# Three passes of a two-layer kernel over token blocks of 384 instead of 288

## The chip, the cores and the metric

One NeuronCore of a Trainium2 chip runs the whole program. The metric is the device time of one execution in microseconds, as the median of several. The core has a matrix engine (TensorE, PE in the profile; its weight loads are listed as PEld), VectorE (DVE), ScalarE (ACT), GpSimd (POOL) and SyncE (SP), which here issues nearly all DMAs.

## The reference

```
attention, B=4, H=8, S=576, D=64, 32 packing queries p per head:
  packed = softmax(p k^T / 8) v          32 x 64 for each head and batch
  x      = softmax(q packed^T / 8) packed          -> 2304 tokens x 512
layer one:  h = x  @ w_in   (512 x 2048);  g = softplus(h);  x1 = g @ w_out   (2048 x 512)
layer two:  h = x1 @ w_in2  (512 x 2048);  g = h*sigmoid(h); y  = g @ w_out2
```

The weights come as 64-bit floats, and the kernel turns them into 32-bit ones from their integer halves. The result is a float32 array of 2304 x 512.

## The kernel before

**Precision.** In most products both operands are split into a rounded part and a remainder (fp32r, one matmul each), and three of the four products are summed: low x high, high x low, high x high.

**Layer one** never builds x. Since x is the second softmax (A, 576 tokens x 32 packing slots x 8 heads, so two row tiles of 128) times `packed`, the kernel multiplies `packed` into w_in first. `packed(b, qs)` makes, for one batch b and some column tiles of w_in, the weights `vw` by small fp32 matmuls (64 x 32 tiles of the array, eight of them side by side, L523) in a two-bank PSUM tile. ScalarE then rounds them out of PSUM (L531) and VectorE makes the remainder (L535). These weights differ from batch to batch. `ax` holds A, rounded and remainder, for all 2304 tokens.

**Passes, units, steps.** The 16 tiles of the hidden dimension (128 each, index j) are taken in four passes of four (`GJ = 4`). In each pass the 2304 tokens are taken in eight blocks of 288, so two blocks make a batch of 576. A unit is one pass and one block, and has four steps, one for each j. A step in `run_steps` does, in this order on TensorE: `emit_in`, the six matmuls of the hidden tile h (L557); a pack call if one is due; `emit_out`, twelve matmuls (L606) that add the unit before, four j times three products, to one of the four 128-row tiles of the output. So every full step has 18 matmuls, each with a 128 x 128 weight load of its own and, for its moving side, the columns of the block. ScalarE takes softplus (L569) and the rounded part gh (L570), VectorE the remainder gl (L574) and the sum of y into `ya` (L622). The hidden tile stays in its PSUM bank until gl is made; there are two such banks.

**What sets the order.** Pass one is a script written out by hand, which also holds the attention. Passes two to four are a loop over steps: 32 a pass, `base(f) = 32 f`. The rest hangs on step numbers in tables: `vstep` says when a pack call runs (for each batch one wide call of 512 columns, two steps ahead of its first block), `when` the conversion of layer one's weights for the next pass, `I2` and `O2` the conversion of layer two's weights, which are made meanwhile and stored to DRAM (`wd`, `od`, `td`), `plan_load` the DMAs at the end of a step. Within a step, `go(point)` lets such jobs put their instructions into each engine's order at a named place (A0 before the step's ScalarE work, A2 behind it, D0, D1, D, D2 on VectorE). Every engine runs its instructions in the order in which they were put, and SP its DMAs likewise.

**Layer two's weights.** A pair of `raw` tiles becomes eight sums in `wf`; `high_i` rounds (L238) and `low_i` (GpSimd, L244) makes remainders into `whl2`, one buffer for all seven products, stored by `store_i` with one DMA of 1792 KB. Output weights go through `ohl` (`high_o`, `low_o`, `store_o`: one DMA of 512 KB) and sums in `tmp` (`t_store`, 1024 KB).

**The change of layers.** From step 24 of the last pass (`XC0`) the staging memory is given up for layer two's operands `xc`, which `x_split` makes from `ya` at steps 24, 25 and 29, its low parts a step later; layer two's first weights are loaded at steps 23 and 24. Layer two (`second`, blocks of 384 tokens) takes the last unit's four output groups into its first step (`last_out`).

Of the kernel before, what the change touches and what calls it, by code (L numbers as in the profile page):

```python
# [28 lines left out]
N0 = 288  # L29
BLOCKS = [(c, N0) for c in range(0, T, N0)]  # L30

# [17 lines left out]
def body(ctx, tc, kT, vv, qT, pT, wi1, wo1, wi2, wo2, out):  # L49
# [5 lines left out]
    dram = pool("dram", 1, space=bass.MemoryType.DRAM)  # L55
    l0_stack, att_stack, stage_stack, psa_stack = (ExitStack() for _ in range(4))
# [456 lines left out]

    def packed(b, qs):
        yield "PE"
        t = two_banks()
        wide = len(qs) > 1
        for k in range(NK):
            w = whl["i", 2 * qs[0] + (k if wide else k // 2)]
            w = w if wide else w[:, (k % 2) * 256:(k % 2 + 1) * 256]  # L520
# [8 lines left out]
        for i, q in enumerate(qs):  # L529
            v = l0.tile([P, 2, NR, 256], F32R, name="vw", bufs=3)  # L530
            nc.scalar.activation(out=v[:, 0], in_=t[:, :, 256 * i:256 * i + 256], func=AF.Copy)  # L531
            vs.append(v)
        yield "D"
        for i, (q, v) in enumerate(zip(qs, vs)):
            nc.vector.tensor_tensor(  # L535
                out=v[:, 1], in0=t[:, :, 256 * i:256 * i + 256], in1=v[:, 0].bitcast(F32), op=ALU.subtract
            )
            vw[b, q] = v

# [3 lines left out]
    def emit_in(s):  # L543
        u, i = steps[s]
        js, blk = units[u]
        j = js[i]
        c, n = BLOCKS[blk]
        cols = slice(c, c + n)
        h = ps.tile([P, 512], F32, name="h")[:, :n]
        v = vw[blk // 2, j // 2]  # L550
        fs = slice((j % 2) * P, (j % 2 + 1) * P)
        mm = [
            (v[:, vp, r, fs], ax[:, ap * NR + r, cols])
            for vp, ap in ((1, 0), (0, 1), (0, 0)) for r in range(NR)
        ]
        for i, (w, x) in enumerate(mm):
            nc.tensor.matmul(h, lhsT=w, rhs=x, start=(i == 0), stop=(i == len(mm) - 1))  # L557
        return h

    def act_scalar(s, h):  # L560
        if s < 2 * GJ:
            gf = g0.tile([P, N0], F32, name="gf", tag="gh")
# [3 lines left out]
        gh = g0.tile([P, N0], F32R, name="gh")  # L566
        gl = g0.tile([P, N0], F32R, name="gl")
# [105 lines left out]

    I2 = (1, 5), (10, 14), (20, 22), (32, 33), (43, 49), (54, 57), (64, 67), (77, 78)
    O2 = 3, 6, 13, 15, 23, 25, 30, 36, 45, 46, 60, 63, 73, 74, 81, 83

    when = {}
    vstep = {(b, (i,)): 8 * b - 4 + i for b in range(B) for i in range(2)}
    vstep[0, (1,)] = 3
    del vstep[0, (0,)]  # L680
    for f in range(1, NPASS):
        for b in range(B):
            vstep[b, (2 * f, 2 * f + 1)] = base(f) + 8 * b - 2

    def last_use(k, n):
        f = n // GJ
        if k == "o":
            return base(f) + PER + GJ
        return vstep[B - 1, (2 * f, 2 * f + 1) if f else (n // 2,)]

    def plan_all():

        for f in range(1, NPASS - 1):
            for d, s in enumerate((7, 9, 26, 29)):
                when["i", GJ * f + GJ + d] = base(f) + s
            for d, s in enumerate((12, 19, 16, 24)):
                when["o", GJ * f + GJ + d] = base(f) + s
        for (k, n), s in when.items():
            ring = RING[k]
            free = last_use(k, n - ring)  # L700
            load = max(s - 5, free)
# [6 lines left out]
        for m, (s, k, n) in enumerate(use):  # L708
            free = use[m - RAW][0] if m >= RAW else 0
            plan_load(lambda k=k, n=n: load_raw(k, n), base(1) + max(free, s - 5))  # L710
        for jp, s in enumerate(I2):
            a, b = (base(1) + x for x in s)
            plan(Item(conv_pair(jp)), (a, b, b + 3, b + 4))
            plan_load(lambda jp=jp: store_i(jp), b + 8)
        for n, s in enumerate(O2):
            s += base(1)
            plan(Item(conv_o(n)), (s, s + 1) + (s + 3,) * (n % 2))
            plan_load(lambda n=n: store_o(n), s + 4)
            if n % 2:
                plan_load(lambda n=n: t_store(n), s + 4)  # L720
        for q, s in (Q1, 24), (Q2, 25), (Q4, 24), (Q5, 25), (Q7, 29), (Q6, 29), (Q3, 29):
            s += base(3)
            plan(Item(x_split(0, q)), (s, s + 1))
        for t in range(RI):
            plan_load(lambda t=t: load_i1(t), base(3) + 23)
        for r in range(GJ):
            plan_load(lambda r=r: load_s(r), base(3) + 24)

# [47 lines left out]
    def first_pass():  # L776
        items, made, ys = {}, {}, {}
        for b in range(B):
            items[f"a1.{b}"] = Item(att1(b))
            for i in range(2):  # L780
                items[f"a2.{2 * b + i}"] = Item(att2(2 * b + i))
                items[f"v.{b}.{i}"] = Item(packed(b, (i,)))
        items["v.0.2.3"] = Item(packed(0, (2, 3)))
        for n in range(2 * GJ):
# [477 lines left out]
```

## Time and profile before

| | |
|---|---|
| median of 3 runs | 724.73 us (724.57 to 725.1) |
| profiled execution | 724.65 us, its span 722.9 us |
| TensorE busy | 716.0 us (99%), 5330 matmuls |
| VectorE, ScalarE, GpSimd busy | 72%, 55%, 55% |
| passes two to four | 117.9 to 361.4 us of the span |
| layer two | from 361.4 us on |

A line of a group gives: source line, engine, operation, output<-input, shape, count, then busy time, the mean duration of one in ns, idle time of the engine just before and what ended it. A timeline line gives the start, how long the merged run of instructions lasted, engine, source line and count. Matmuls are pipelined: one starts before the one ahead has ended, so that spacing is read from the starts of neighbours and not from durations.

### The profile page before, as it was taken

How to read it: one execution, taken by the hardware profiler on the slowest of the kernel's cores; microseconds unless marked ns; L12 is line 12 of the kernel's file. 1: busy time of each engine (PE TensorE's matmuls, PEld its weight loads, DVE VectorE, ACT ScalarE, POOL GpSimd, SP SyncE). 2: the span in 40 equal slices, each digit the busy share in tenths (PEclk: the TensorE clock that was granted, in tenths of full speed). 3: DMA queues.
4: the chain of work that ended last, by engine and by line, in shares of the span. 5: the costliest groups of instructions: out<-in, count | busy, mean ns of one | idle time of the engine just before them, and what ended most of it. 6: DMA issues, size and time to landing. Idle time of an engine off the chain costs nothing.

```text
span 722.9 us, 14127 instructions
## 1 busy us (share of the span) xinstructions
PE 716.0 (99%) x5330; PEld 685.5 (95%) x5330; DVE 520.7 (72%) x937; ACT 394.3 (55%) x789; POOL 397.5 (55%) x352
## 2 busy tenths in 40 slices
PE   8999999999999999999999999999999999999998
PEld 6878999999899999999999999999999999999997
DVE  4888888888878887575845567787557786645557
ACT  3677887767765766556636534443644363444341
POOL 0122110857753746456027567689656769765655
PEclk9999999999999999999999999999999999999999
DMA  9946151587687664485739878778978787987732
GB/s 337 365 166 228 69 193 39 197 328 302 261 318 269 241 244 194 146 306 220 261 124 315 276 240 269 247 245 279 313 258 262 238 269 239 307 301 243 252 120 101
DMA packets 78915, 173.15 MB, mean 240 GB/s; under 512 B 6400, under 2 KB 52992, under 8 KB 76288
## 3 DMA queue, kind: packets, MB, share of 16 engines
q1 hardware_dynamic: 78704, 172.19, 69.1%
q8 instruction: 42, 0.69, 0.4%
q14 instruction: 25, 0.20, 0.1%
q10 hardware_dynamic: 144, 0.07, 0.0%
HBM read 136.05 MB, written 36.18 MB: 238 GB/s over the span
## 4 chain that ended last, share of the span: by engine, by line
PE 91%; DVE 4%; ACT 3%; issue 1%; DMA 1%; POOL 0%; DVEq 0%; ACTq 0%
PE y L964 23%; PE y L606 23%; PE h L557 13%; PE pB L907 7%; PE pA L907 7%; PE pC L907 7%; PE pD L907 3%; PE y L599 2%; PE psa L523 2%; PE psa L425 1%; PE y L739 1%; PE psa L377 1%; PE psa L477 1%; DMA pz<-pT 1%; DVE raw L212 1%
## 5 line engine op out<-in xcount | busy, mean ns | idle before, releaser
L606 PE MATMUL y<-gh,w 128*128 128x288 f32 x960 | 211.0, 296 | 0.0
L606 PEld LDWEIGHTS y<-gh,w 128*128 128x128 f32 x960 | 160.2, 188 | 11.1 <-issue 10.2
L964 PE MATMUL y<-G,w 128*128 128x384 f32 x840 | 164.4, 334 | 0.1
L964 PEld LDWEIGHTS y<-G,w 128*128 128x128 f32 x840 | 147.3, 188 | 0.5 <-DVE acc L979 0.5
L606 PE MATMUL y<-gl,w 128*128 128x288 f32 x480 | 141.4, 295 | 0.0
L557 PE MATMUL h<-ax,vw 128*128 128x288 f32 x768 | 123.4, 297 | 0.0
L557 PEld LDWEIGHTS h<-ax,vw 128*128 128x128 f32 x768 | 108.3, 188 | 3.4 <-issue 1.8
L946 POOL TENSOR_TENSOR G<-sums,G 128x384 fp32r<-128x384 f32 x76 | 87.9, 1179 | 35.4 <-ACT G L942 21.3
L938 POOL TENSOR_TENSOR sums<-tmp 128x384 f32<-128x384 f32 x47 | 56.5, 1225 | 91.6 <-ACT tmp L1151 90.3
L606 PEld LDWEIGHTS y<-gl,w 128*128 128x128 f32 x480 | 90.1, 188 | 0.0
L574 DVE TENSOR_TENSOR gl<-h,gh 128x288 fp32r<-128x288 f32 x100 | 45.1, 451 | 30.8 <-ACT gh L570 30.7
L569 ACT ACTIVATE h<-h 128x288 f32<-128x288 f32 x100 | 39.0, 390 | 47.0 <-PE h L557 45.5
L1147 ACT ACTIVATE tmp<-tmp 128x384 f32<-128x384 f32 x24 | 12.6, 526 | 79.8 <-DVE tmp L1078 79.8
L1078 DVE TENSOR_TENSOR tmp<-tmp,pB 128x384 f32<-128x384 f32 x48 | 26.4, 550 | 40.0 <-PE pB L907 34.8
L622 DVE TENSOR_TENSOR ya<-y,ya 128x288 f32<-128x288 f32 x104 | 46.7, 450 | 10.6 <-PE y L606 9.8
L1078 DVE TENSOR_TENSOR G<-tmp,G 128x384 fp32r<-128x384 f32 x61 | 45.5, 746 | 11.1 <-ACT G L1152 5.5
L1107 ACT ACTIVATE tmp<-pA 128x384 f32<-128x384 f32 x24 | 11.8, 492 | 68.3 <-PE pA L907 68.3
L907 PE MATMUL pB<-xc,w 128*128 128x384 f32 x240 | 48.1, 334 | 0.0
L907 PE MATMUL pC<-xc,w 128*128 128x384 f32 x240 | 48.1, 334 | 0.0
L979 DVE TENSOR_TENSOR ya<-y,ya 128x384 f32<-128x384 f32 x70 | 38.4, 553 | 11.1 <-PE y L964 10.8
L1078 DVE TENSOR_TENSOR tmp<-tmp,pC 128x384 f32<-128x384 f32 x48 | 26.5, 553 | 25.9 <-PE pC L907 24.9
L570 ACT ACTIVATE gh<-h 128x288 fp32r<-128x288 f32 x100 | 41.2, 412 | 3.2
(155 smaller groups left out, 1371.0 us busy)
## 6 DMA issues: line engine op xcount, KB each, us to landing
w<-wd SPq DMA_DIRECT2D x84, 512.0 KB, 4.4
w<-td SPq DMA_DIRECT2D x96, 256.0 KB, 3.6
w<-od SPq DMA_DIRECT2D x72, 256.0 KB, 3.8
wd<-whl SPq DMA_DIRECT2D x8, 1792.0 KB, 9.2
wraw<-wi SPq DMA_DIRECT2D x16, 512.0 KB, 7.9
wraw<-wo SPq DMA_DIRECT2D x16, 512.0 KB, 8.6
raw<-wi SPq DMA_DIRECT2D x16, 512.0 KB, 6.5
raw<-wo SPq DMA_DIRECT2D x16, 512.0 KB, 5.8
```

The costliest lines, as they stand in the source:

```text
L557: nc.tensor.matmul(h, lhsT=w, rhs=x, start=(i == 0), stop=(i == len(mm) - 1))
L569: nc.scalar.activation(out=gt, in_=h, func=AF.Softplus)
L570: nc.scalar.activation(out=gh, in_=gt, func=AF.Copy)
L574: (engine("gl", s) if s < IN_BANK else nc.vector).tensor_tensor(out=gl, in0=gt, in1=gh.bitcast(F32), op=ALU.subtract)
L606: nc.tensor.matmul(y, lhsT=w[:, c], rhs=g, start=(j == js[0] and m == 0), stop=(j == js[-1] and m == 2))
L622: nc.vector.tensor_tensor(out=acc, in0=y, in1=acc, op=ALU.add)
L907: nc.tensor.matmul(out, lhsT=a, rhs=b, start=start and not i, stop=not start and i == len(mm) - 1, skip_group_check=True,)
L938: eng.tensor_tensor(out=sum_of(q), in0=a, in1=b, op=op)
L946: eng.tensor_tensor(out=u[:, 1], in0=sum_of(q), in1=u[:, 0].bitcast(F32), op=ALU.subtract)
L964: nc.tensor.matmul(y, lhsT=w, rhs=g, start=not m, stop=m == len(mm) - 1)
L979: vec = lambda o, x, z, op=ALU.add: nc.vector.tensor_tensor(out=o, in0=x, in1=z, op=op)
L1078: add = lambda o, i, j, op=ALU.add: nc.vector.tensor_tensor(out=o, in0=i, in1=j, op=op)
```

## The change

Pass one keeps its eight blocks of 288. Passes two to four run over six blocks of 384, so a pass has 24 steps. Blocks 0 and 2 of each three lie inside one batch; the middle one takes its first 192 tokens from one batch and its last 192 from the next. There `emit_in` does six matmuls of 192 columns with each batch's weights, into the two halves of h. The weights of batches 0 and 2 still come from one wide pack call, those of 1 and 3 from three, of 256, 128 and 128 columns, at three different steps. All tables of steps are set anew for 24 steps a pass; the gh and gl buffers grow to 384 columns; layer two's staged weights go through a smaller buffer in two parts of four and three products, each with a store of its own, and output rows through three half-size buffers with two stores.

```diff
 N0 = 288
-BLOCKS = [(c, N0) for c in range(0, T, N0)]
+N2 = 384
+FIRST_PASS = T // N0
+BLOCKS = [(c, N0) for c in range(0, T, N0)] + [(c, N2) for c in range(0, T, N2)]
...
-    cp = push(l0_stack, "cp", 2, side="right")
     l0 = push(l0_stack, "l0", 1, side="right")
-    wp5 = push(l0_stack, "wp5", 1, side="right")
     g0 = push(l0_stack, "g0", 2 * GJ + 1, side="right")
+    cp = push(conv_stack, "cp", 2, side="right")
+    wp5 = push(conv_stack, "wp5", 1, side="right")
...
-    units += [(group(f), blk) for f in range(NPASS) for blk in range(0 if f else 2, len(BLOCKS))]
+    units += [(group(0), blk) for blk in range(2, FIRST_PASS)]
+    units += [(group(f), blk) for f in range(1, NPASS) for blk in range(FIRST_PASS, len(BLOCKS))]
...
-    PER = GJ * len(BLOCKS)
-    base = lambda f: f * PER
+    PER = GJ * (len(BLOCKS) - FIRST_PASS)
+    base = lambda f: GJ * FIRST_PASS + (f - 1) * PER if f else 0
...
-        st["parts"] = ((0, NQ),)
+        st["parts"] = (0, 4), (4, NQ)
...
     def store_o(n):
-        w = o_hl.pop(n)
-        nc.sync.dma_start(
-            out=od[:, n * 2 * DM:(n + 1) * 2 * DM], in_=w.bitcast(F32).rearrange("p h n -> p (h n)")
-        )
+        for h, w in enumerate(o_hl.pop(n)):
+            c = (2 * n + h) * DM
+            nc.sync.dma_start(out=od[:, c:c + DM], in_=w.bitcast(F32))
...
-    def packed(b, qs):
+    def packed(b, js):
         yield "PE"
         t = two_banks()
-        wide = len(qs) > 1
+        n, c = len(js) * P, js[0] % GJ * P
         for k in range(NK):
...
+                w = whl["i", js[0] // GJ * GJ + k][:, c:c + n]
...
-                    t[32 * k:32 * k + 32, r, :512 if wide else 256], lhsT=pts[b][rows, k * NP:(k + 1) * NP],
+                    t[32 * k:32 * k + 32, r, :n], lhsT=pts[b][rows, k * NP:(k + 1) * NP],
...
         h = ps.tile([P, 512], F32, name="h")[:, :n]
-        v = vw[blk // 2, j // 2]
-        fs = slice((j % 2) * P, (j % 2 + 1) * P)
-        mm = [
-            (v[:, vp, r, fs], ax[:, ap * NR + r, cols])
-            for vp, ap in ((1, 0), (0, 1), (0, 0)) for r in range(NR)
-        ]
-        for i, (w, x) in enumerate(mm):
-            nc.tensor.matmul(h, lhsT=w, rhs=x, start=(i == 0), stop=(i == len(mm) - 1))
+        for b in range(c // S, (c + n - 1) // S + 1):
+            lo, hi = max(c, b * S), min(c + n, b * S + S)
+            v = vw[b, j]
+            mm = [
+                (v[:, vp, r], ax[:, ap * NR + r, lo:hi])
+                for vp, ap in ((1, 0), (0, 1), (0, 0)) for r in range(NR)
+            ]
+            for i, (w, x) in enumerate(mm):
+                nc.tensor.matmul(h[:, lo - c:hi - c], lhsT=w, rhs=x, start=(i == 0), stop=(i == len(mm) - 1))
         return h
...
     for f in range(1, NPASS):
         for b in range(B):
-            vstep[b, (2 * f, 2 * f + 1)] = base(f) + 8 * b - 2
+            j, s = GJ * f, base(f) + GJ * (3 * b // 2)
+            if b % 2:
+                vstep[b, (j, j + 1)], vstep[b, (j + 2,)], vstep[b, (j + 3,)] = s - 2, s, s + 1
+            else:
+                vstep[b, group(f)] = s - 2
...
-            for d, s in enumerate((7, 9, 26, 29)):
+            for d, s in enumerate((7, 9, 20, 21)):
                 when["i", GJ * f + GJ + d] = base(f) + s
-            for d, s in enumerate((12, 19, 16, 24)):
+            for d, s in enumerate((12, 14, 15, 17)):
                 when["o", GJ * f + GJ + d] = base(f) + s
...
-            plan(Item(conv_pair(jp)), (a, b, b + 3, b + 4))
-            plan_load(lambda jp=jp: store_i(jp), b + 8)
+            plan(Item(conv_pair(jp)), (a, b, b + 2, b + 5))
+            plan_load(lambda jp=jp: store_i(jp, 0), b + 4)
+            plan_load(lambda jp=jp: store_i(jp, 1), b + 6)
...
-            plan_load(lambda n=n: store_o(n), s + 4)
+            plan_load(lambda n=n: store_o(n), s + 2)
...
-        for q, s in (Q1, 24), (Q2, 25), (Q4, 24), (Q5, 25), (Q7, 29), (Q6, 29), (Q3, 29):
+        for q, s in (Q1, 19), (Q2, 19), (Q4, 18), (Q5, 19), (Q7, 22), (Q6, 22), (Q3, 22):
...
-    XC0 = 24
+    XC0 = 18
```

## Rows read from the trace of the kernel before

**Rows 1.** The page: engine totals, chain of waits by engine.
```profile
PE 716.0 (99%) x5330; PEld 685.5 (95%) x5330; DVE 520.7 (72%) x937; ACT 394.3 (55%) x789; POOL 397.5 (55%) x352
...
PE 91%; DVE 4%; ACT 3%; issue 1%; DMA 1%; POOL 0%; DVEq 0%; ACTq 0%
```

**Rows 2.** Windows: busy PE, PEld, DVE, ACT, POOL (instructions), granted clock, DMA share, GB/s.
```profile
117.90:361.44 243.54, 243.49 (x1907) 231.33 (x1905) 192.06 (x371) 157.65 (x324) 136.64 (x114) 1.00 0.66 247
...
380.00:700.00 320.00, 320.00 (x1847) 319.85 (x1847) 210.06 (x339) 143.10 (x283) 226.96 (x199) 1.00 0.82 262
```

**Rows 3.** Timeline of TensorE, 319.6 to 340 us: hidden matmuls and a wide pack call.
```profile
319.65 0.96 PE L557 MATMUL h<-ax,vw 128*128 128x288 f32 x6
...
336.32 0.96 PE L557 MATMUL h<-ax,vw 128*128 128x288 f32 x6
...
339.93 0.29 PE L557 MATMUL h<-ax,vw 128*128 128x288 f32 x1
```

**Rows 4.** Groups of weight loads by shape, whole span (mean ns behind the comma).
```profile
L964 PEld LDWEIGHTS y<-G,w 128*128 128x128 f32 x840 | 147.3, 188 | 0.5 <-DVE acc L979 0.5
L557 PEld LDWEIGHTS h<-ax,vw 128*128 128x128 f32 x768 | 108.3, 188 | 3.4 <-issue 1.8 <-DVE gl L574 0.5 <-ACT gh L570 0.5
...
L411 PEld LDWEIGHTS psa<-ident,e 128*128 128x128 f32 x32 | 3.8, 141 | 1.2 <-ACT e L402 0.9
...
L411 PEld LDWEIGHTS psa<-ident,e 128*64 128x64 f32 x8 | 0.9, 111 | 0.0
```

**Rows 5.** Timeline of weight loads: a warm-up run and a run of transposes.
```profile
15.74 3.20 PEld L739 LDWEIGHTS y<-ident 128*128 128x128 f32 x28 [0.41 <-issue]
...
26.93 1.11 PEld L411 LDWEIGHTS psa<-ident,e 128*128 128x128 f32 x10
```

**Rows 6.** Timeline of TensorE in pass one: a pack call of 256 columns.
```profile
39.75 1.06 PE L557 MATMUL h<-ax,vw 128*128 128x288 f32 x6
...
41.33 2.21 PE L599 MATMUL y<-gf,wraw 128*128 128x288 f32 x8
```

**Rows 7.** Timeline of TensorE around a wait at a pack call.
```profile
193.59 0.96 PE L557 MATMUL h<-ax,vw 128*128 128x288 f32 x6
...
198.01 0.96 PE L557 MATMUL h<-ax,vw 128*128 128x288 f32 x6
```

**Rows 8.** Groups of the page: evictions at 288 and 384 columns.
```profile
L574 DVE TENSOR_TENSOR gl<-h,gh 128x288 fp32r<-128x288 f32 x100 | 45.1, 451 | 30.8 <-ACT gh L570 30.7
...
L979 DVE TENSOR_TENSOR ya<-y,ya 128x384 f32<-128x384 f32 x70 | 38.4, 553 | 11.1 <-PE y L964 10.8
```

**Rows 9.** DMA issues of passes two to four: size, median us to landing.
```profile
wd<-whl SPq DMA_DIRECT2D x8, 1792.0 KB, 9.2
...
td<-tmp SPq DMA_DIRECT2D x8, 1024.0 KB, 5.0
```

**Rows 10.** Groups of ScalarE and GpSimd, passes two to four: layer two's staged weights.
```profile
L238 ACT ACTIVATE whl<-wf 128x1024 fp32r<-128x1024 f32 x8 | 8.4, 1054 | 0.0
L238 ACT ACTIVATE whl<-wf 128x768 fp32r<-128x768 f32 x8 | 6.7, 838 | 0.0
...
L244 POOL TENSOR_TENSOR whl<-wf,whl 128x1024 fp32r<-128x1024 f32 x8 | 19.8, 2473 | 6.4 <-ACT whl L238 6.4
```

**Rows 11.** Timeline: ScalarE and VectorE on one hidden tile.
```profile
302.77 0.40 ACT L569 ACTIVATE h<-h 128x288 f32<-128x288 f32 x1 [0.81 <-PE h L557]
...
303.64 0.46 DVE L574 TENSOR_TENSOR gl<-h,gh 128x288 fp32r<-128x288 f32 x1 [1.21 <-ACT gh L570]
```

**Rows 12.** Waits of SP's queue, passes two to four: us, times, longest.
```profile
SPq L278 <- POOL ohl L274: 52.4, 12, 13.0
```

**Rows 13.** Timeline around the change of layers: low parts, and Q6's first matmuls.
```profile
358.42 2.69 DVE L660 TENSOR_TENSOR xc<-ya,xc 128x768 fp32r<-128x768 f32 x3
...
362.49 1.20 PE L907 MATMUL pB<-xc,w 128*128 128x384 f32 x6
```

**Rows 14.** Group of TensorE in pass one: plain fp32 products.
```profile
L599 PE MATMUL y<-gf,wraw 128*128 128x288 f32 x64 | 17.5, 414 | 0.0
```

More of the change, by code (lines that the diff above doesn't have):

```diff
@@ L55, in body @@
     dram = pool("dram", 1, space=bass.MemoryType.DRAM)
-    l0_stack, att_stack, stage_stack, psa_stack = (ExitStack() for _ in range(4))
+    l0_stack, conv_stack, att_stack, stage_stack, psa_stack = (ExitStack() for _ in range(5))
     push = lambda stack, name, bufs, **kw: stack.enter_context(tc.tile_pool(name=name, bufs=bufs, **kw))
     pool("edge", 1, side="right").tile([P, 88], F32, name="edge")
-    cp = push(l0_stack, "cp", 2, side="right")
     l0 = push(l0_stack, "l0", 1, side="right")
-    wp5 = push(l0_stack, "wp5", 1, side="right")
     g0 = push(l0_stack, "g0", 2 * GJ + 1, side="right")
+    cp = push(conv_stack, "cp", 2, side="right")
+    wp5 = push(conv_stack, "wp5", 1, side="right")
     att = push(att_stack, "att", 1)
@@ L512, in body @@
     vw = {}
-    def packed(b, qs):
+    def packed(b, js):
         yield "PE"
         t = two_banks()
-        wide = len(qs) > 1
+        n, c = len(js) * P, js[0] % GJ * P
         for k in range(NK):
-            w = whl["i", 2 * qs[0] + (k if wide else k // 2)]
-            w = w if wide else w[:, (k % 2) * 256:(k % 2 + 1) * 256]
+            if js[0] < GJ:
+                w = whl["i", js[0] + k // 2][:, (k % 2) * 256:(k % 2 + 1) * 256]
+            else:
+                w = whl["i", js[0] // GJ * GJ + k][:, c:c + n]
             for r in range(NR):
@@ L528, in packed @@
         vs = []
[L529 to L532, printed above, removed]
+        for i in range(0, n, 256):
+            m = min(n, 256)
+            if len(js) == 1 and js[0] % GJ == 2:
+                v = st["tp"].tile([P, 2, NR, P], F32R, name="vj")
+            else:
+                v = l0.tile([P, 2, NR, 256], F32R, name="vw", bufs=3)[:, :, :, :m]
+            nc.scalar.activation(out=v[:, 0], in_=t[:, :, i:i + m], func=AF.Copy)
+            vs.append((i, m, v))
         yield "D"
-        for i, (q, v) in enumerate(zip(qs, vs)):
+        for i, m, v in vs:
             nc.vector.tensor_tensor(
-                out=v[:, 1], in0=t[:, :, 256 * i:256 * i + 256], in1=v[:, 0].bitcast(F32), op=ALU.subtract
+                out=v[:, 1], in0=t[:, :, i:i + m], in1=v[:, 0].bitcast(F32), op=ALU.subtract
             )
-            vw[b, q] = v
+            for x in range(0, m, P):
+                vw[b, js[(i + x) // P]] = v[:, :, :, x:x + P]
     gs = {}
@@ L561, in act_scalar @@
         if s < 2 * GJ:
-            gf = g0.tile([P, N0], F32, name="gf", tag="gh")
+            gf = g0.tile([P, N2], F32, name="gf", tag="gh")[:, :N0]
             nc.scalar.activation(out=gf, in_=h, func=AF.Softplus)
@@ L565, in act_scalar @@
             return None
-        gh = g0.tile([P, N0], F32R, name="gh")
-        gl = g0.tile([P, N0], F32R, name="gl")
+        n = BLOCKS[units[steps[s][0]][1]][1]
+        gh = g0.tile([P, N2], F32R, name="gh")[:, :n]
+        gl = g0.tile([P, N2], F32R, name="gl")[:, :n]
         gt = h if s >= IN_BANK else att.tile([P, N0], F32, name="gt", bufs=2)
@@ L615, in finish_out @@
         acc = ya[:, dm, c:c + n]
-        if u == FIRST[blk]:
+        if blk < FIRST_PASS and u == FIRST[blk]:
             if 4 * u + dm in BY_SCALAR:
@@ L671, in x_split @@
         x_low(s, q)
-    I2 = (1, 5), (10, 14), (20, 22), (32, 33), (43, 49), (54, 57), (64, 67), (77, 78)
-    O2 = 3, 6, 13, 15, 23, 25, 30, 36, 45, 46, 60, 63, 73, 74, 81, 83
+    I2 = (1, 2), (8, 10), (16, 18), (24, 25), (32, 34), (42, 43), (50, 51), (58, 59)
+    O2 = 4, 6, 11, 13, 19, 22, 27, 30, 35, 40, 46, 48, 53, 56, 61, 63
     when = {}
-    vstep = {(b, (i,)): 8 * b - 4 + i for b in range(B) for i in range(2)}
-    vstep[0, (1,)] = 3
-    del vstep[0, (0,)]
+    vstep = {(b, (2 * i, 2 * i + 1)): 8 * b - 4 + i for b in range(B) for i in range(2)}
     for f in range(1, NPASS):
         for b in range(B):
-            vstep[b, (2 * f, 2 * f + 1)] = base(f) + 8 * b - 2
+            j, s = GJ * f, base(f) + GJ * (3 * b // 2)
+            if b % 2:
+                vstep[b, (j, j + 1)], vstep[b, (j + 2,)], vstep[b, (j + 3,)] = s - 2, s, s + 1
+            else:
+                vstep[b, group(f)] = s - 2
     def last_use(k, n):
@@ L700, in plan_all @@
             free = last_use(k, n - ring)
-            load = max(s - 5, free)
+            load = max(s - 4, free)
             assert load <= s - 3, (k, n, s, load)
@@ L709, in plan_all @@
             free = use[m - RAW][0] if m >= RAW else 0
-            plan_load(lambda k=k, n=n: load_raw(k, n), base(1) + max(free, s - 5))
+            plan_load(lambda k=k, n=n: load_raw(k, n), base(1) + max(free, s - 4))
         for jp, s in enumerate(I2):
             a, b = (base(1) + x for x in s)
-            plan(Item(conv_pair(jp)), (a, b, b + 3, b + 4))
-            plan_load(lambda jp=jp: store_i(jp), b + 8)
+            plan(Item(conv_pair(jp)), (a, b, b + 2, b + 5))
+            plan_load(lambda jp=jp: store_i(jp, 0), b + 4)
+            plan_load(lambda jp=jp: store_i(jp, 1), b + 6)
         for n, s in enumerate(O2):
             s += base(1)
-            plan(Item(conv_o(n)), (s, s + 1) + (s + 3,) * (n % 2))
-            plan_load(lambda n=n: store_o(n), s + 4)
+            plan(Item(conv_o(n)), (s, s + 1) + (s + 2,) * (n % 2))
+            plan_load(lambda n=n: store_o(n), s + 2)
             if n % 2:
-                plan_load(lambda n=n: t_store(n), s + 4)
-        for q, s in (Q1, 24), (Q2, 25), (Q4, 24), (Q5, 25), (Q7, 29), (Q6, 29), (Q3, 29):
+                plan_load(lambda n=n: t_store(n), s + 3)
+        for q, s in (Q1, 19), (Q2, 19), (Q4, 18), (Q5, 19), (Q7, 22), (Q6, 22), (Q3, 22):
             s += base(3)
@@ L724, in plan_all @@
         for t in range(RI):
-            plan_load(lambda t=t: load_i1(t), base(3) + 23)
+            plan_load(lambda t=t: load_i1(t), base(3) + 18)
         for r in range(GJ):
-            plan_load(lambda r=r: load_s(r), base(3) + 24)
+            plan_load(lambda r=r: load_s(r), base(3) + 18)
         for (b, qs), s in vstep.items():
@@ L781, in first_pass @@
                 items[f"a2.{2 * b + i}"] = Item(att2(2 * b + i))
-                items[f"v.{b}.{i}"] = Item(packed(b, (i,)))
-        items["v.0.2.3"] = Item(packed(0, (2, 3)))
+                items[f"v.{b}.{i}"] = Item(packed(b, (2 * i, 2 * i + 1)))
+        items["v.0.2.3"] = Item(packed(0, group(1)))
         for n in range(2 * GJ):
@@ L813, in run_steps @@
                 att_stack.close()
-                st["tmp"] = pool("tmp", 1, reuse_waits="tile").tile([P, 8 * N1], F32, name="tmp")
+                st["tp"] = pool("tmp", 1, reuse_waits="tile")
+                st["tmp"] = st["tp"].tile([P, 8 * N1], F32, name="tmp")
                 open_stage()
@@ L821, in run_steps @@
                 close_stage()
+                conv_stack.close()
                 open_xc()
```

10 lines of the change are left out of this document (5 added, 5 removed).

## The prediction

> **What bounds the kernel now.** I read the page first: TensorE is busy for 99% of the span, and the chain of waits that ended last is 91% TensorE [rows 1]. Next comes a table of windows. Passes two to four of layer one run from 117.90 to 361.44 us, and there TensorE is busy for all but 0.05 us of the 243.54, at full granted clock, while VectorE has 79%, ScalarE 65% and GpSimd 56% [rows 2]. So the stage is set by how many instructions TensorE gets, and at what spacing. An engine beside it matters only if it makes TensorE wait.
>
> Spacing then has to be read from starts, since a matmul's own duration overlaps with the next one's. In the timeline of TensorE each step begins with its six hidden-layer matmuls. From 319.65 to 336.32 there are seven steps, so one step of 18 matmuls of 288 columns takes 2.381 us, or 132.3 ns each [rows 3]. At 384 columns layer two gives the price: 1847 matmuls in 320.00 us, 173.3 ns each, at full clock too [rows 2]. The columns alone would be 120 and 160 ns at 2.4 GHz; each matmul has 12 to 13 ns on top, at both widths. The step with a wide pack call is 339.93 - 336.32 = 3.61 us, so a wide call costs 1.23 us that nothing covers [rows 3].
>
> The old stage adds up: 96 x 2.381 = 228.6, 11 wide calls (a twelfth is in pass one's script) x 1.23 = 13.5, together 242.1 of 243.54. The last 1.4 us are short waits, 0.81 of them in the step from 193.59 to 198.01, which is longer by that than others with a wide call [rows 7].
>
> **The change, part by part.**
>
> *Fewer, wider matmuls.* Three passes have 24 units of 4 steps before and 18 after. The columns streamed are the same; what can be saved is the 12 to 13 ns per matmul. Of the 72 new steps 48 belong to blocks inside one batch: 18 x 173.3 = 3.120 us, 149.8 us in all. The other 24 belong to the two middle blocks of each pass. Their 12 output matmuls cost 12 x 173.3 = 2.080 us, but the hidden layer there needs twelve matmuls of 192 columns, six with each batch's weights, in place of six.
>
> *The price of a 192-column matmul* is the disputed number, as the trace has none. From below: its columns are 80 ns. By the straight line through 288 and 384 it is 132.3 - 41.0 = 91.3 ns. But each matmul also brings a weight load. A load's duration depends on its kind: 111 ns for 64 columns and 141 for 128 in the attention's transposes, 188 for the 128 columns of this kernel's fp32r weights, whether the matmul behind it has 288 or 384 columns [rows 4]. From 111 to 141 is about 27 ns more for 64 more columns, one column a cycle; 188 is 47 to 50 more again, what another 128 cycles would take. So I estimate that an fp32r load occupies its path for some 256 cycles, 107 ns. Behind 288 columns (120 ns) that is hidden, behind 192 (80 ns) it isn't. The nearest row is the warm-up: 128-column matmuls with loads of about the same length, 0.19 us, follow each other at (3.20 - 0.19) / 27 = 111.5 ns [rows 5]. I take 112 ns. From above: 107 plus the same 13 gives 120, and rival three has more. A spanning step is then 2.080 + 12 x 0.112 = 3.424 us, 82.2 us for 24. Sum 232.0 against 228.6: **+3.4 us** (-2.6 at 91.3 ns, +5.7 at 120).
>
> The Trainium skill, "TensorE: Matmul & The Clock Gate", section "LDWEIGHTS", says that a load's time goes by its columns, P/1.2 ns, which is 107 ns for 128. That speaks against the change, and the warm-up row agrees with it; by 107 instead of 112 the sum would be 1.4 us lower.
>
> *Pack calls.* The old kernel makes the weights of each batch and pass in one wide call. The new one does that for batches 0 and 2; for 1 and 3 it makes three calls, of 256, 128 and 128 columns. A 256 call is in pass one: from the step at 39.75 to the next work at 41.33 are 1.58 us, of which six matmuls at 132 ns are 0.79, so the call costs 0.79 [rows 6]. Two calls give a line: (1.23 - 0.79) / 256 = 1.7 ns a column, and 0.36 fixed. A 128 call is then 0.79 - 0.22 = 0.57 us (bounds: half of the 256 call, 0.40, and all of it, 0.79). An odd batch costs 0.79 + 2 x 0.57 = 1.93 against 1.23, so 6 x 0.70 = **+4.2 us** (+2.2 to +6.8). Nothing covers it: the call stands in TensorE's order behind the step's hidden matmuls. It needs the one pack bank back, for which the call of the step before must have been copied; that copy has a step of over 3 us.
>
> *Work beside it.* Evictions become wider and fewer: a piece on VectorE goes from 451 ns at 288 columns to some 553 at 384, two a step, so 96 x 2 x 451 = 86.6 us become 72 x 2 x 553 = 79.6; ScalarE's two a step go the same way [rows 8]. No engine comes nearer to being the bound. This is worth nothing while TensorE does not wait.
>
> *Layer two's weights.* The staged block is stored in two parts through one buffer, so ScalarE's second rounding, three steps behind the first, waits for the first part's store to land. Counting from the step of the first: ScalarE comes to it at about 2.3 us, takes 1.05, GpSimd 2.47, a store of 1 MB lands in 5.0, together 10.8; the second is reached at 3 x 3.12 + 2.3 = 11.7 [rows 9, 10]. About 1 us is left, less what GpSimd and SP are behind. Behind a waiting rounding stand the next softplus and the gl subtraction. The hidden bank that they free is wanted two steps later, 6.24 us, and from the end of the hidden matmuls the three together take 302.77 to 304.10, 1.3 us, now and some 1.6 wide; the bank is written for 1.0 to 1.3 us first, so they have about 3.5 us of play [rows 11]. I cost it at 0, with rival four for the cover gone. The output rows are stored in halves, 16 more issues of a third of a us on SP, and sooner behind GpSimd; SP already waits 52 us for GpSimd there without any harm that TensorE shows [rows 12]. Cost 0, bounds 0 and a us.
>
> *The end of the stage.* Layer two's last three operand sums are rounded in the last step but one, and their low parts made in the last; both were one step further ahead. VectorE now begins them at 358.42, 0.95 each, so the second, Q6, is done by 360.3 and wanted at 362.49 [rows 13]. The lead shrinks from two steps of 2.38 to one of 3.12, by 1.64 us, and 0.5 remains. Cost 0, up to 1 us if VectorE is late. Step 0 of layer two gets 48 matmuls of 384 instead of 288 columns (+2.0 us), and the first four steps of pass two still have 288 (-2.0): the sum above is for all units, wherever they run.
>
> *Sum.* 3.4 + 4.2 = +7.6 us, the old 1.4 us of waits kept. The profiled execution took 724.65 us (span 722.87 and 1.8 around it), the median is 724.73, 0.08 away. 724.65 + 7.6 = **732.3 us**. Own range with the bounds of load, packing and waits: 728 to 737.
>
> **Rivals.**
>
> *Two, the load stays hidden (91.3 ns).* Then 288 narrow matmuls cost 6.0 us less: +1.6, 726.3 us. For it: both measured widths lie on one line. Against: the load durations and the 112 ns row. The same page's section "Back-to-back issue gap" gives 81 ns at 128 columns and 131 at 512 for a stream of loads and matmuls; between them I estimate 89 ns here, 725.7 us. The trace disagrees with that rule: on its line 384 columns would be at 114 ns, and the row has 173.
>
> *Other side, the narrow matmul costs its columns alone (80 ns)*, in the 24 spanning steps: 288 x 32 ns = 9.2 us less, -1.6 and 723.1 us, faster. It decides from a spacing of 112 - 7.6/0.288 = 85.6 ns down. For it: the transposes run at (1.11 - 0.14) / 9 = 108 ns with 128 columns, so some of the 12 ns may go with the kind of matmul [rows 5]. Against: both fp32r widths carry them.
>
> *Three, a narrow fp32r matmul doesn't stream a column a cycle.* The plain fp32 matmuls of pass one cost 17.5 us / 64 = 273 ns per instruction of 288 columns, two per product [rows 14]. One such pass pair at 192 columns would be 182 ns: +20 us, 752. Both: 365 ns, +73, 805. For it: no fp32r matmul under 288 columns has been seen here. Against: nothing in the rows ties the rate to width.
>
> *Four, ScalarE is held by the first part's store.* If that lands only as the whole block does now, 9.2 us instead of 5.0 [rows 9], ScalarE waits 3.3 us and the step behind it, with 0.84 more for the rounding [rows 10], is about 4.1 late against 3.5 of play; with GpSimd's queue 1.5 us more behind, TensorE loses 2 us in each of eight pairs: 16 us, 748.
>
> **How the numbers follow.** Forecast 0.64; load hidden 0.13; columns alone 0.05; narrow and slow 0.10; held by the store 0.08. About 0.2%, 1.45 us, is what can be told from no change. Faster: the 0.05 and a little of the hidden load, 0.06. Same, 723.3 to 726.2: near half of the hidden load, 0.06. Slower: 0.88. The range 725.5 to 741 holds the forecast's own, most of the hidden load and the mild end of rival four, about 0.8.
>
> **What would show it.** Starts of the hidden matmuls in the middle blocks 112 ns apart (91 for rival two, 80, or over 150); steps of 3.12 and 3.42 us; pack calls of 128 columns 0.57 us each; the stage from 117.90 on about 6 us longer, and layer two's first step 2 us. The prediction is wrong if the narrow spacing is under 100 ns, if TensorE has waits of more than 2 us in sum behind gl or ScalarE, or if the odd batches' calls are covered.

## The result, and the profile after

The changed kernel takes 732.75 us (median of four, 732.62 to 733.15), the kernel before 724.91 us beside it (724.57 to 725.53): ratio 1.0108, 95% interval 1.0091 to 1.0126. It is slower by 7.8 us. Its profiled span is 730.9 us, 8.0 longer than before.

The page after, its engines and its chain of waits, to be read against [rows 1]:

```profile
PE 723.6 (99%) x5234; PEld 692.0 (95%) x5234; DVE 523.6 (72%) x895; ACT 387.6 (53%) x747; POOL 396.0 (54%) x352
...
PE 93%; DVE 2%; POOL 1%; ACT 1%; DMA 1%; issue 1%; SPq 0%; POOLq 0%; DVEq 0%; ACTq 0%
```

There are 96 TensorE instructions fewer, and TensorE is busy 7.6 us longer. VectorE has 42 instructions fewer and is busy 2.9 us longer all the same, ScalarE 6.7 us less. Passes two to four as one window, against the first line of [rows 2] (us, then busy time and instructions of PE, PEld, DVE, ACT and POOL, granted clock, DMA share, GB/s):

```profile
118.23:366.66 248.43, 248.01 (x1810) 234.94 (x1809) 193.77 (x329) 150.97 (x282) 135.07 (x114) 1.00 0.66 242
```

The stage is 4.9 us longer, TensorE waits 0.4 us in it, and the granted clock is full, as before. So the loss there is work of TensorE, not waiting. Its price is read from the timeline of TensorE, here the hidden matmuls (L567) and the pack calls (L528) of the last pass (start, length of the merged run, count), against [rows 3]:

```profile
325.98 1.21 PE L567 MATMUL h<-ax,vw 128*128 128x384 f32 x6
...
329.10 1.21 PE L567 MATMUL h<-ax,vw 128*128 128x384 f32 x6
...
332.23 1.22 PE L567 MATMUL h<-ax,vw 128*128 128x384 f32 x6
333.38 0.66 PE L528 MATMUL psa<-wraw,pt 64*32 64x256 f32 x16
...
336.16 1.21 PE L567 MATMUL h<-ax,vw 128*128 128x384 f32 x6
...
339.28 1.48 PE L567 MATMUL h<-ax,vw 128*128 128x192 f32 x12
340.69 0.45 PE L528 MATMUL psa<-wraw,pt 64*32 64x128 f32 x16
...
343.27 1.48 PE L567 MATMUL h<-ax,vw 128*128 128x192 f32 x12
344.68 0.45 PE L528 MATMUL psa<-wraw,pt 64*32 64x128 f32 x16
...
347.26 0.81 PE L567 MATMUL h<-ax,vw 128*128 128x192 f32 x6
347.90 0.83 PE L567 MATMUL h<-ax,vj 128*128 128x192 f32 x6
348.58 0.36 PE L617 MATMUL y<-gh,w 128*128 128x384 f32 x1
...
350.72 1.48 PE L567 MATMUL h<-ax,vw 128*128 128x192 f32 x12
...
354.16 1.21 PE L567 MATMUL h<-ax,vw 128*128 128x384 f32 x6
```

Twelve matmuls of 192 columns take from 347.26 to 348.58: 110 ns each. A step inside one batch takes 3.12 to 3.13 us (325.98 to 329.10 to 332.23), a spanning one 3.46 and 3.44 (347.26 to 350.72 to 354.16). A 256 call adds 3.93 - 3.13 = 0.80 us, a 128 call 3.99 - 3.46 = 0.53. These are the steps and calls that the working had priced.

The one wait of ScalarE that rival four was about, and the only wait of TensorE's matmuls that the view of waits names in the stage (us in total, times, longest):

```profile
ACT whl L241 <- DMA wd<-whl: 1.8, 1, 1.8
...
PE psa L528 <- DVE vj L544: 0.4, 1, 0.4
```

And the two stores of the staged weights, against [rows 9] (count, KB each, median us to landing):

```profile
wd<-whl SPq DMA_DIRECT2D x8, 1024.0 KB, 4.3
...
wd<-whl SPq DMA_DIRECT2D x8, 768.0 KB, 3.4
```

### The profile page after: what moved, and what is told of

Its sections match the earlier page's. It is cut to its first block, busy times and chain, and to the rows that moved or that the text cites. A ratio compares the mean times of both kernels' runs of the same rounds, so it can differ in the third digit from the quotient of the medians.

```text
span 730.9 us, 13897 instructions
## 1 busy us (share of the span) xinstructions
PE 723.6 (99%) x5234; PEld 692.0 (95%) x5234; DVE 523.6 (72%) x895; ACT 387.6 (53%) x747; POOL 396.0 (54%) x352
## 2 busy tenths in 40 slices
DMA packets 82371, 173.14 MB, mean 237 GB/s; under 512 B 6784, under 2 KB 53376, under 8 KB 79744
## 4 chain that ended last, share of the span: by engine, by line
PE 93%; DVE 2%; POOL 1%; ACT 1%; DMA 1%; issue 1%; SPq 0%; POOLq 0%; DVEq 0%; ACTq 0%
PE y L617 24%; PE y L980 23%; PE h L567 13%; PE pB L923 7%; PE pA L923 7%; PE pC L923 7%; PE pD L923 3%; PE y L610 2%; PE psa L528 2%; PE y L753 1%; DMA td<-tmp 1%; PE psa L428 1%; PE psa L380 1%; PE psa L480 1%; PE psa L414 0%
## 5 line engine op out<-in xcount | busy, mean ns | idle before, releaser
L617 PE MATMUL y<-gh,w 128*128 128x384 f32 (+1 forms) x768 | 203.0, 329 | 0.0
L617 PEld LDWEIGHTS y<-gh,w 128*128 128x128 f32 x768 | 137.1, 188 | 10.9 <-issue 10.0
L617 PE MATMUL y<-gl,w 128*128 128x384 f32 (+1 forms) x384 | 125.0, 325 | 0.0
L567 PE MATMUL h<-ax,vw 128*128 128x384 f32 (+2 forms) x696 | 113.6, 304 | 0.0
L567 PEld LDWEIGHTS h<-ax,vw 128*128 128x128 f32 x696 | 102.8, 189 | 2.9 <-issue 1.8
L617 PEld LDWEIGHTS y<-gl,w 128*128 128x128 f32 x384 | 72.1, 188 | 0.0
L580 ACT ACTIVATE h<-h 128x384 f32<-128x384 f32 (+1 forms) x76 | 35.5, 467 | 63.8 <-PE h L567 59.4
L585 DVE TENSOR_TENSOR gl<-h,gh 128x384 fp32r<-128x384 f32 (+1 forms) x76 | 41.5, 546 | 27.3 <-ACT gh L581 27.3
L633 DVE TENSOR_TENSOR ya<-y,ya 128x384 f32<-128x384 f32 (+1 forms) x80 | 43.2, 542 | 22.5 <-PE y L617 21.7
L288 POOL TENSOR_TENSOR tmp<-tmp 128x256 f32<-128x256 f32 x32 | 24.1, 764 | 42.8 <-DVE tmp L218 42.2
L1094 DVE TENSOR_TENSOR tmp<-tmp,pC 128x384 f32<-128x384 f32 x48 | 26.5, 553 | 25.4 <-PE pC L923 24.4
```

The lines of the kernel that those rows point to most:

```text
L288: sub = lambda o, a, b: nc.gpsimd.tensor_tensor(out=o, in0=a, in1=b, op=ALU.subtract)
L567: nc.tensor.matmul(h[:, lo - c:hi - c], lhsT=w, rhs=x, start=(i == 0), stop=(i == len(mm) - 1))
L585: (engine("gl", s) if s < IN_BANK else nc.vector).tensor_tensor(out=gl, in0=gt, in1=gh.bitcast(F32), op=ALU.subtract)
L617: nc.tensor.matmul(y, lhsT=w[:, c], rhs=g, start=(j == js[0] and m == 0), stop=(j == js[-1] and m == 2))
L1094: add = lambda o, i, j, op=ALU.add: nc.vector.tensor_tensor(out=o, in0=i, in1=j, op=op)
```

## The experiments

Ratios are to the kernel before, which took 724.6 to 725.1 us beside them, with their 95% interval.

**What sets the spacing of a narrow matmul: e3 and e5.** e3 does the blocks inside one batch in 256 and 128 columns too; e5 does the middle blocks' narrow matmuls with 64 of the 128 weight columns, behind six wide ones.

```diff
# e3
+        cuts = [c, c + 256, c + n] if first == last and n > N0 else ...
+        for lo, hi in zip(cuts, cuts[1:]):
# e5
...
+        six(first, c, c + n, P)
+        if first < last:
+            six(first, c, last * S, 64)
+            six(last, last * S, c + n, 64)
```

> The changed kernel, with the hidden layer of the other blocks cut too, into 256 and 128 columns with the same weights loaded twice. Theory, spacing is the larger of the load, 111, and 0.427 ns a column + 9.3: 119 ns at 256, 111 at 128, the same as at 192; steps of 3.47 instead of 3.13, 48 of them, 749 us. Rival, spacing follows columns at all widths and 192 is dear for another reason: 119 and 64 ns, steps of 3.18, 735 us.

> The changed kernel, with the middle blocks' hidden tile made by six matmuls of 384 columns with the first batch's weights, and its first 64 rows then made again by twelve matmuls of 192 columns with 64 weight columns each; the second batch's weights are left out for the other 64 rows. Theory, the narrow matmul waits for its load, and a load of 64 columns takes half, some 53 ns: spacing falls from 111 to the line's 91 ns; 24 steps of 4.2 us. Rival, 192 moving columns cost 111 ns whatever is loaded: spacing stays at 111, steps of 4.45.

e3 took 747.94 us, one run. Hidden matmuls and the first output matmul behind them in its timeline of TensorE:

```profile
323.42 1.48 PE L568 MATMUL h<-ax,vw 128*128 128x256 f32 x12
324.74 0.39 PE L618 MATMUL y<-gh,w 128*128 128x384 f32 x1
```

These twelve are six of 256 and six of 128 columns, 1.32 us together, as much as twelve of 192 in the kernel after. Read start by start, the medians are 118 ns at 256 columns and 111 at 192 and at 128: from 192 to 128 columns nothing more is saved. Only the second matmul of a run comes sooner, 88 ns behind the first at 192 columns in the kernel after and 59 at 128 in e3, both with 128 weight columns: ahead of it stands a wider matmul, under which the loads keep up. From then on the loads themselves start 109 to 112 ns apart (read from 347.26 to 348.49 in the kernel after). In e5 (751.41 us, one run) six narrow matmuls with 64-column weights:

```profile
320.71 0.69 PE L568 MATMUL h<-ax,vj 128*64 128x192 f32 x6
321.24 0.36 PE L623 MATMUL y<-gh,w 128*128 128x384 f32 x1
```

0.53 / 6 = 88 ns, median 89 over the run. The moving side is the same 192 columns; the weight load is half, and so are the rows of the output, but the 88 ns of the second matmul above came with all 128. The view of weight loads says by how much (busy us, mean ns):

```profile
L568 PEld LDWEIGHTS h<-ax,vw 128*128 128x128 f32 x366 | 64.8, 188 | 0.0
...
L568 PEld LDWEIGHTS h<-ax,vw 128*64 128x64 f32 x234 | 22.7, 135 | 0.9
```

So at 192 columns the load is the bound; that is shown. With half of it the spacing is 80 ns of columns and 9 on top. The Trainium skill, "TensorE: Matmul & The Clock Gate", section "LDWEIGHTS", gives a load 107 ns for 128 columns and 53 for 64: the 53 ns between the two rows and the floor of 111 agree with it.

**How much of the loss is the narrow matmuls: e2.** The middle blocks take six matmuls of 384 columns, all with the first batch's weights.

```diff
-        for b in range(c // S, (c + n - 1) // S + 1):
-            lo, hi = max(c, b * S), min(c + n, b * S + S)
+        for b in range(c // S, c // S + 1):
+            lo, hi = c, c + n
```

> The changed kernel, with the hidden layer of the middle blocks as six matmuls of 384 columns with the first batch's weights; what is left out is the second batch's weights for its 192 tokens. Theory, a narrow matmul takes 111 ns as its weight load isn't hidden: 24 steps go from 12 x 111 to 6 x 173.5 ns, 0.29 us each, 7.0 us in all: 725.7 us. Rival, the narrow ones cost 91 ns and the loss lies elsewhere: 24 x (1.10 - 1.04) = 1.3 us, 731.4.

Measured 726.7 us (726.35 to 726.9), ratio 1.0025 (1.0015 to 1.0034): 6.0 us less than the kernel after. Each of 24 steps is 3.13 in place of 3.45 us, 7.7 together; 1.2 are lost as steps with waits grow, most of it where TensorE waits for VectorE's copy of a pack (0.4 us in the kernel after), and 0.5 stay unexplained; in the timeline of TensorE:

```profile
175.55 0.45 PE L528 MATMUL psa<-wraw,pt 64*32 64x128 f32 x16 [1.17 <-DVE vj L544]
```

**How much is the packing: e1 and e6.** Both give the odd batches one wide call again. e1 makes room for that by two raw buffers in place of three and by eight gh and gl buffers; e6 keeps the three and puts gh and gl into one arena of eight places, with ScalarE's gh put behind the output matmuls; pass one's first eight hidden tiles are rounded to fp32r for it.

```diff
-                vstep[b, (j, j + 1)], vstep[b, (j + 2,)], vstep[b, (j + 3,)] = s - 2, s, s + 1
...
+            vstep[b, group(f)] = s - 2
# e1 alone
-RAW = 3
+RAW = 2
...
# e6 alone
+    arena = [g0.tile([P, NG], F32R, name=n) for n in ("gh", "gl")]
...
+            ys = emit_out(s)
             r = act_scalar(s, h)
-            ys = emit_out(s)
```

> The changed kernel with one wide pack call for batches 1 and 3 too, as for 0 and 2 (room for it: two raw buffers instead of three, eight gh and gl buffers instead of nine). Theory, the small calls cost 1.86 us per odd batch against 1.22 for a wide one and nothing covers them: six odd batches give back 6 x 0.64 = 3.8 us, 732.7 to 728.9 us, still slower than the kernel before by 4 us. Rival, the calls lie in time that TensorE would lose anyway: no change, 732.7. Second rival, the taken-away buffers cost waits: the calls go as foretold in the trace, the time stays above 730, and gaps between matmuls appear elsewhere.

> The changed kernel with wide pack calls for all batches, and the three raw buffers kept: room comes from gh and gl in one tile each for two units, a step's output group put ahead of its rounding in the order, and pass one's first eight hidden tiles rounded to fp32r. Theory, the small calls cost 1.86 us per odd batch, a wide one 1.22: 3.8 us back, 728.9 us, and what the run with two raw buffers lost above that was its waits alone. Rival, the calls' cost moves into a new wait, as the weights come in one lump: above 731.

e1: 736.04 us (735.67 to 736.26), ratio 1.0155 (1.0142 to 1.0169), slower than the kernel after, as its second rival had it. From pass three on its wide calls cost 1.22 us as foretold, but a buffer fewer holds up SP. First the kernel after, then e1, in the queue waits of SP:

```profile
SPq L255 <- POOL whl L247: 80.6, 15, 11.6
SPq L204 <- DVE tmp L218: 41.9, 9, 10.1
SPq L204 <- DVE wf L218: 35.1, 7, 24.3
```

```profile
SPq L204 <- DVE wf L218: 81.0, 15, 29.7
SPq L204 <- DVE tmp L218: 65.5, 13, 10.3
SPq L255 <- POOL whl L247: 38.5, 8, 9.3
```

L204 is the load of a raw tile, L255 the store of the staged weights behind it in the same order. The load now waits for its buffer twice as long, 147 us in place of 77, the store goes late, and ScalarE's rounding, which needs the store's buffer, waits 9.7 us where it had waited 1.8:

```profile
ACT whl L241 <- DMA wd<-whl: 9.7, 3, 4.3
```

Beside one of these waits, and beside TensorE's longest, the timeline has:

```profile
147.03 0.85 ACT L241 ACTIVATE whl<-wf 128x768 fp32r<-128x768 f32 x1 [4.26 <-DMA wd<-whl]
...
151.38 1.32 PE L567 MATMUL h<-ax,vj 128*128 128x384 f32 x6 [1.24 <-DVE gl L585]
```

```profile
174.05 2.44 DVE L166 TENSOR_SCALAR wx<-wraw 128x512 int32<-128x512 int32 x1
...
178.53 2.54 PE L567 MATMUL h<-ax,vw 128*128 128x192 f32 x12 [1.77 <-DVE gl L585]
```

The first pair is rival four's mechanism, brought about by another cause: the late rounding makes softplus, gh and gl late, and the same happens once more at 208 us. The two cost TensorE 3.2 of the 7.5 us by which e1's steps exceed others of their kind. Another 3.6 stand in the two steps from 173.14 on, where no store is waited for: a shift of VectorE ahead of gl took 2.44 us, of which more below. e6 took 730.87 us (730.29 to 731.23), ratio 1.0081 (1.0067 to 1.0094). Its undisturbed stretch of twelve steps takes 41.25 us (269.82 to 311.07) against 41.91 (312.25 to 354.16) after: 0.66 us for each odd batch, 4.0 for six. It lost 2.1 of that again and so lies between its theory and its rival; 1.9 are waits in pass two (2.5 us where the kernel after has 0.6), most in one wide call that waited for VectorE in the middle:

```profile
192.66 1.07 PE L529 MATMUL psa<-wraw,pt 64*32 64x512 f32 x12
194.76 1.05 PE L529 MATMUL psa<-wraw,pt 64*32 64x512 f32 x4 [1.02 <-DVE wraw L173]
```

**A version without narrow matmuls: e4 and e7.** Blocks of 320, 512 and 320: the middle one does 256 columns of either batch. e7 is e6 with these blocks; e4 is an earlier form with e1's buffers, in which each unit's last output group reads a hidden tile that had been overwritten.

```diff
-N2 = 384
+N2 = 320
+NM = 2 * S - 2 * N2
-BLOCKS = ... + [(c, N2) for c in range(0, T, N2)]
+BLOCKS = ... + [(c + o, n) for c in range(0, T, 2 * S) for o, n in ((0, N2), (N2, NM), (N2 + NM, N2))]
```

> Blocks of 320, 512 and 320 tokens in place of 384, so that the middle one has 256 tokens of each batch; wide pack calls for all batches; gh and gl in one tile each, and pass one's first eight hidden tiles rounded to fp32r for it. Theory: from 256 columns up the load is hidden and a matmul is at 0.427 ns a column + 9.3: 146 ns at 320, 228 at 512, 119 at 256. Steps 2.63 and 4.16 us, 6 x (8 x 2.63 + 4 x 4.16) = 225.8 against 228.6 before, packing as before: 724.7 - 2.8 = 721.9 us, faster than both. Rival, the load needs more than 107 ns behind a stream, say 133: 288 x 14 ns more, 726. Rival, evictions of 512 columns keep the two hidden banks too long: steps of 320 behind them lengthen, over 724.

> As the run before, with blocks of 320, 512 and 320 tokens, so that the hidden matmuls of the middle block have 256 columns. Theory: at 256 columns the load is hidden (118 ns seen), 320 and 512 cost 146 and 228 ns; passes two to four 225.8 us of matmuls against 228.6 before and 232.4 in the changed kernel, packing as before: 721.9 us, faster than both. Rival, waits: the evictions of 512 columns and the uneven steps keep TensorE waiting for ScalarE, as in the run with two raw buffers; then above 724.

e4: 762.8 us (759.37 to 765.01), ratio 1.0524. All waits of TensorE that its view names in passes two to four are output matmuls waiting for gh, 26.5 us; behind the longest, 6.1 us, ScalarE had waited 4.4 us for the late store. e7: 728.84 us (728.25 to 729.54), ratio 1.0053 (1.004 to 1.0065). It beats the kernel after and not the one before; its expectation was 6.9 us too low, and its rival, waits, held. Undisturbed, twelve steps take 40.13 us (227.35 to 267.48) against 16 x 2.381 + 2 x 1.22 = 40.54 before, so over six such stretches only 2.5 us are gained. That counts the last unit too, whose 12 matmuls of 512 and 48 of 320 columns, in place of 60 of 288, fall into layer two and make its first steps 1.9 longer and the stage as much shorter. Against the gain stand 0.9 for a wait in layer two that ends at 596.2 us, 0.2 for a later start of pass two, 0.4 more behind the last matmul and 0.9 spread over layer two, the last three not explained. And 5.3 us of waits, 1.4 before, stand in pass two, nearly all between 169 and 198 us:

```profile
173.91 1.68 PE L569 MATMUL h<-ax,vw 128*128 128x256 f32 x12 [1.34 <-DVE gl L595]
...
194.48 1.05 PE L530 MATMUL psa<-wraw,pt 64*32 64x512 f32 x4 [0.81 <-DVE wraw L174]
```

VectorE is 92 to 93% busy there (third busy time of the windows):

```profile
168.00:182.00 14.00, 12.54 (x93) 12.02 (x92) 12.87 (x19) 9.18 (x17) 9.48 (x7) 1.00 0.67 239
182.00:200.00 18.00, 16.33 (x95) 12.62 (x94) 16.70 (x27) 9.78 (x20) 9.99 (x11) 1.00 0.68 239
```

**Whether VectorE's shifts are what is late: e8 to e12.** The shift of a weight conversion takes 0.42 us at the least, and up to 2.6 in pass two of e7. In e8, e9 and e10 (e7, after, before) it became an operation with two SBUF sources; in e11 and e12 (e7, before) the second source is the scaled word in PSUM.

```diff
-        nc.vector.tensor_scalar(out=x, in0=lw, scalar1=29, ..., op0=ALU.logical_shift_right)
# e8, e9, e10
+            zero = edge.bitcast(I32)[:, :1].to_broadcast([P, DM])
+            nc.vector.scalar_tensor_tensor(
+                out=x, in0=lw, scalar=29, in1=zero, op0=ALU.logical_shift_right, op1=ALU.bitwise_or
...
# e11, e12
+            nc.vector.scalar_tensor_tensor(
+                out=x, in0=lw, scalar=29, in1=hw, op0=ALU.logical_shift_right, op1=ALU.bitwise_xor
...
```

> As e7 (blocks of 320, 512 and 320), but from pass two on the first shift of each weight conversion is an operation of another kind with the same result. Ground: e7 lost 5.3 us to waits of TensorE, all between 169 and 198 us, where VectorE is 92 to 93% busy; its shift (one source, 128x512) takes 0.42 us alone, but up to 2.60 there, mean 0.74 and 0.85, while the two-source operations of the same tiles beside it take 0.69 every time. Theory: the long shifts make the gl behind them late, so a shift of fixed length takes the long waits away although VectorE's total stays as it is: waits of 2 us or less in that stretch, time 723.6 to 725.5. Rival: VectorE's total load is the limit there; then the waits stay near 5 us and the time is 728 to 729.

> The changed kernel with the same edit of the shift alone. Its waits in passes two to four are 0.6 us. If the prediction's accounting holds, nothing else can be gained: 732.2 to 732.8, not distinguishable from the changed kernel. Rival: waits of VectorE hide elsewhere (start of the passes, layer two's first step), and it falls by over 1 us, below 731.7.

> The kernel before with the same edit of the shift alone. Its waits in passes two to four are 1.4 us, 0.8 of them in one step behind a wide pack call. Theory: most of these go, 723.5 to 724.5. Rival: they aren't from the shift (the wait is for the store or the load of a weight), 724.9.

> As e7 (blocks of 320, 512 and 320), with the shift of each conversion from pass two on written so that its second source is the word that lies in PSUM (the low bits are combined with it by exclusive or, and the next operation takes it out again; the same three operations, the same result). In the runs so far every operation of VectorE with a source in PSUM took 0.69 us whatever GpSimd did, while shifts with SBUF sources alone took 0.42 to 2.60 (one source) and 0.68 to 2.37 (two). Theory: it is the PSUM source that keeps an operation out of GpSimd's way: 50 shifts at 0.69, 34.6 us in place of 38.9, none above 0.8; waits of TensorE from 169 to 198 us fall from 5.3 to 2 or less, time 724 to 726. Rival: the shift must now wait for ScalarE's scaling, which cost VectorE 0.8 us each time already, so VectorE is as late as before: 728 or more, with new waits of the shift for ScalarE.

> The kernel before with the same edit of the shift. Theory: no shift above 0.8 us, VectorE 4.6 us busier (34.6 us of shifts in place of 30.0), the wait of 0.8 us at 193.59 gone: 724 to 725, no difference that can be told. Rival: as with two SBUF sources, where 13 us more of shifts cost 4.8 us of time, the time goes by VectorE's total: 4.6 us more cost 1.7, 726.7.

e8 took 734.83 us (ratio 1.0133, 1.0119 to 1.0147), e9 737.57 (1.0174, 1.016 to 1.0188), e10 729.88 (1.0069, 1.0055 to 1.0083): none of the three expectations held, theory or rival, since I had taken any two-source operation for one of fixed length. The shifts grew instead, in e10 (lines of VectorE, 118 to 361 us) to means of 0.81 and 0.98, where the kernel before has 0.58 and 0.64; those that read x, which lies in PSUM, stay at a mean of 0.69:

```profile
L157 DVE SCALAR_TENSOR_TENSOR raw<-raw,edge 128x512 int32<-128x512 int32 x32 | 25.8, 807 | 0.0
L222 DVE SCALAR_TENSOR_TENSOR raw<-x,raw 128x512 int32<-128x512 int32 x32 | 22.2, 693 | 3.8 <-ACT x L148 0.6
L157 DVE SCALAR_TENSOR_TENSOR wx<-wraw,edge 128x512 int32<-128x512 int32 x18 | 17.7, 982 | 0.0
```

GpSimd's 128x1024 remainders grow in the same run, from 2473 ns [rows 10] to 2572. The Trainium skill, "SBUF — State Buffer", section "Who interferes with whom", says that an operation of VectorE with two SBUF inputs contends with a GpSimd instruction that reads SBUF, and one with a single SBUF input outside the fast modes doesn't; the rows, means over the passes, agree.

e11 took 730.45 us (1.0077, 1.0064 to 1.0091), e12 735.15 (1.0141, 1.0127 to 1.0155). Now the lengths came as the theory said, but for some in e12 of up to 0.92 us; e12 in the lines of VectorE:

```profile
L156 DVE SCALAR_TENSOR_TENSOR raw<-raw,x 128x512 int32<-128x512 int32 x32 | 22.5, 704 | 6.9 <-ACT x L147 6.6
...
L156 DVE SCALAR_TENSOR_TENSOR wx<-wraw,x 128x512 int32<-128x512 int32 x18 | 12.3, 683 | 5.9 <-ACT x L147 3.9 <-POOL tmp L297 1.1 <-POOL w L198 0.5
```

but not the times: e11's agrees with its rival, and e12's lies beyond both its theory and its rival. The shift had been done while ScalarE scaled the other word, and now waits for it (6.6 and 3.9 us). In e11 the waits of pass two did fall, from 5.3 to 2.3 us, but others came: 2.0 us in the step at 126.85, 1.6 from 263 to 279. In e12 TensorE waits for gl where the kernel before hardly waited at all:

```profile
PE h L569 <- DVE gl L586: 6.7, 11, 0.8
```

It isn't VectorE's total that decides: e10 has 13.5 us more of shifts than the kernel before and loses 4.8 us, e12 has 4.8 us more (34.8 for 30.0) and loses 10.5. What fits both is when gl comes, as a conversion that ends later in its step delays the gl behind it; that reading was not tested by itself. Whether another order of the conversions would let e7 fall below the kernel before wasn't tried.

## Why the prediction was right

The forecast was 732.3 us, the measured median 732.75. By its own steps:

- *What bounds.* TensorE's own instructions, in the profile after as before; neither VectorE nor ScalarE costs over 0.6 us. Right.
- *The narrow matmul, 112 ns.* 110 to 111, and e5 with e3 shows that the load is the cause, as argued from the durations [rows 4] and the warm-up [rows 5]. Rival two (91.3) and the other side (80) fall with it; e5's 88, with half the load, is what they would have needed. Rival three falls too: 192 columns cost no more than 88 ns where the load allows.
- *The matmul term, +3.4.* Too small. Twelve steps without their calls take 41.91 - 1.22 - 0.80 - 2 x 0.53 = 38.83 us against 16 x 2.381 = 38.10: 0.73, and six times that is +4.4. The steps are 0.01 (384) and 0.03 (spanning) longer than forecast; in the spanning ones the first matmul behind the twelve takes 200 ns in place of 173.
- *Packing, +4.2.* 0.80 + 2 x 0.53 - 1.22 = 0.64 for an odd batch, +3.8; the 128 call measured 0.53 for 0.57. e6 gets 0.66 a batch back where nothing waits. Nothing covers the calls: right.
- *Waits.* I kept the old 1.4 us; 0.6 are left, -0.8, counted as what steps exceed others of their kind by. Of these, 0.4 is a wait for a pack's copy, for which I had counted on a step of over 3 us. One cause of the old ones, the long step at 193.59 [rows 7], has 0.11 of excess in its place. Why it shrank wasn't tested.
- *The staged block in two parts, 0.* Right: ScalarE waited once, 1.8 us, and TensorE never for it. The store landed in 4.3 us, not the 5.0 assumed. e1 shows that the cover is thin.
- *Work beside it.* VectorE's gl and sums into `ya` shrank by 7 us over the span, as forecast, but its shifts grew in passes two to four from 30.0 to 35.8 us, which the working had left out; TensorE's waits fell all the same.
- *The change of layers.* I counted 48 wider matmuls in layer two's first step; 60 output matmuls of the last unit fall behind its first matmul, 2.5 us in place of 2.0, and the stage has that half microsecond less. No wait for late operands was seen.

Sum: 4.4 + 3.8 - 0.8 = 7.4 of the 8.0 us. The rest is pass two starting 0.33 us later and 0.3 us more behind the last matmul; neither was predicted or tested. So the mechanism is shown, and three sizes were off by 1.0, -0.4 and -0.8 that nearly cancel: the half microsecond of agreement is luck.

## What to carry to other kernels

Before cutting moving tiles to fit a boundary, price the narrow matmul by its weight load, not by its columns: below the width at which the load is hidden, narrower saves nothing. A split call pays its fixed cost again, here some 0.3 us each. And a buffer taken away to make room is paid for in an in-order queue: look at what stands behind the transfer that now waits.

## What the runs showed of the hardware

- fp32r matmuls with 128 x 128 weights, start to start in a run at granted clock 1.00: 111 ns at 128 and at 192 columns, 118 at 256, 132 at 288, 173 at 384; with 64 weight columns, 89 at 192.
- An operation of VectorE on 128x512 words with a source in PSUM took 0.69 us nearly always and 0.95 at the most (e1), beside the same work of GpSimd; with SBUF sources alone 0.41 to 2.60 (e7) with one, 0.68 to 2.85 (e8) with two.
